# Attention and two feed-forward layers on one core: keys in groups of two token tiles, split left-over tokens, and a re-planned instruction order

## The chip, the cores and the metric

The kernel runs on one core of a Trainium2 chip. The metric is the time of one execution in device microseconds, lower is better; a kernel's time is the median of its runs. The profile is one execution, recorded by the hardware. In it PE is TensorE, PEld its weight loads, DVE VectorE, ACT ScalarE, POOL GpSimd, and SP the engine that issues most DMAs.

## The reference

Four batches, eight heads, 576 tokens, head size 64; then 2304 tokens of width 512 through two feed-forward layers of width 2048. Everything is float32.

```python
def phi(x):                                  # w_phi is 64 x 128
    proj = np.einsum('bhsd,df->bhsf', x, w_phi)
    proj = proj - np.max(np.abs(proj), axis=-1, keepdims=True)
    return np.concatenate([np.exp(proj), np.exp(-proj)], axis=-1)
q_p, k_p = phi(q), phi(k)
kv = np.einsum('bhsf,bhsd->bhfd', k_p, v);  z = np.sum(k_p, axis=2)
num = np.einsum('bhsf,bhfd->bhsd', q_p, kv)
den = np.einsum('bhsf,bhf->bhs', q_p, z)[..., None] + 1e-06
x = (num / den) as 2304 x 512
x = leaky_relu(x @ w_in1, 0.01) @ w_out1     # first layer
x = relu(x @ w_in2) ** 2 @ w_out2            # second layer
```

## The kernel before

**Number formats.** A product that needs float32 accuracy is made in one of two ways. *Plain*: one float32 matmul, which the trace shows as two records of the PE. *Split*: both operands are cut into a rounded "high" and a "low" part of type float32r, and three matmuls (high·high, low·high, high·low) replace the plain one. Layers one and two are split throughout; in the attention, `P["pk"]`, `P["pq"]` and `P["pn"]` say up to which batch the K projection, the Q projection and the numerator stay plain (0, 0 and 1). The products of K features with V ("kv") are always plain.

**Attention.** Work goes by pairs of heads, four pairs in a batch. `k_pair` loads a pair's keys (512 tokens of two heads stacked on 128 partitions, `kt`; the 64 left-over tokens of each head as one 64 x 128 tile, `krt`) and values (`vt`). It then passes over five groups: the left-over tile (number 4, one head's width of 128 columns for both heads) and the token tiles 0 to 3 (two heads, 256 columns). For each group PE projects into a PSUM bank (`proj`), DVE takes the largest magnitude of every row and negates it (`center`, tile `kmx`), ACT makes exp of the projection and of its negative, one instruction per head and sign, straight from the bank (`expo`, tile `kp`), and PE multiplies by V into the pair's accumulator (`kv`, bank 0, or 0 and 7 in batch 0). After batch 0 the K projections have one bank, number 1; the Q projections and numerators use banks 1 and 0. The accumulator is copied out (`kvf`) and split (`kvh`, `kvl`). `q_pair` does 288 query tokens of a pair: projection for each head (`proj`), copy out of the bank (`qps`), a largest magnitude over partitions on POOL (`qm`), exponentials (`qe`, split into `qeh` and `qel`), numerators and denominators of both heads (`numer`), evacuation (`qnum`, `qden`), reciprocal, product and split into the input `xr` of layer one.

**Layer one** runs over five blocks of tokens (four of 512, one of 256) and 16 chunks of the width 2048 (`moe`): twelve up-projection matmuls into bank 2 or 3 (`xr` with the weights in `arena` or `more`), leaky relu and split on ACT and DVE (`g`, `gh`, `gl`), and twelve down-projection matmuls into banks 4 to 7. The attention of batch b+1 is worked in between the chunks of earlier blocks. While these run, DVE and ACT also turn the weights, which arrive as 64-bit words, into split float32 (`raw`, `wf`), and prepare the second layer's weights (`stage_pair`). **Layer two** follows on PE alone with its own block scheme (`h_unit`, `y_unit`).

**What sets the order.** No engine is ordered by hand. Every piece of work is an `Op` of a `Plan`, with a cost for each engine that may do it, a position `pos`, and its operands. `Plan.order` plays these costs through: a free engine takes the ready operation with the smallest position whose tiles and banks are free. The instructions are then issued in the order in which the play started them, and each engine of the chip works through its list in that order. The positions come from the table `P`: `k0`, `kz`, `kp`, `ks`, `kvd` and others say where a K pair, its tiles and its kv products stand relative to the chunks; `stage0`, `stage`, `lead` and the like where weights are prepared. Between the end of an operation and the start of one that depends on it the play lays `lat`, 0.28, and nothing on the same engine:

```python
for o in op.next:
    t = now + (0.0 if op.engine in o.engines and len(o.engines) == 1 else self.lat)
```

While the play finds nothing for PE in the first 95 us (`fill`), it puts a small bfloat16 matmul on a tile of zeros there, whose result is not used.

Of the kernel before, what the change touches and what calls it, by code (L numbers as in the profile page):

```python
# [19 lines left out]
PAIRS = H // 2  # L20
# [23 lines left out]
EDGE = 24  # L44

P = dict(
    ring=6, wf=2, raws=3, k0=-115.69, kz=(-22.16, -25.13, -28.64), kp0=14.6, kp=22.44, ks=1.84, kvd=6.19, kb=0, pk=0, pq=0, pn=1, qk=2.73, qk2=13.5,
    q20=-8.75, qd=(3.27, -21.24, 20.79, 10.82, -2.12, -17.72, 26.78), wlead=30.91, wl0=-7.1, ydelay=16.3, xs=(174.51, 74.74, 10.17), xl=11.4, xk=4.78,
    xk2=8.22, xst=74.82, xld=24.14, lead=43.44, slead=-24.15, w2lead=29.72, ylead=53.84, evac=-12.29, stage0=-99.0, stage=14.29, stage2=-10.59,
    pl=-1.44, c_alt=43.95, sq_alt=7.93, klead=27.27, qlead=25.53, hi_alt=0.31, dve_alt=34.87, port=1.25, lat=0.28, issue=0.47, dma=2.5, rate=320e3,  # L50
    kvc=0.9, fill=95, cold=4.98, coldf=2.2,
# [29 lines left out]
class Plan:  # L81
# [30 lines left out]

    def order(self, filler=None):
        now, n_done, seq, port = 0.0, 0, 0, 0.0
# [6 lines left out]

        def make_ready(op):
            for e, (_, extra) in op.engines.items():
                heapq.heappush(ready[e], (op.pos + extra, id_of[op], op))
# [19 lines left out]
        while n_done < len(self.ops):  # L144
            for e in free:
                while free[e] <= now:
                    skipped, found = [], None
                    while ready[e]:
                        item = heapq.heappop(ready[e])
                        op = item[2]  # L150
                        if op.engine:
                            continue
                        if can(op):
                            found = op
                            break
                        skipped.append(item)
                    for item in skipped:
                        heapq.heappush(ready[e], item)
# [25 lines left out]
                    if e == "PE" and now < P["cold"]:  # L184
                        cost *= P["coldf"]
# [8 lines left out]
            while events and events[0][0] <= now:  # L194
                _, _, what, op = heapq.heappop(events)
                if what == "end":
                    n_done += 1
                    seq += 1
                    heapq.heappush(events, (now + self.lat, seq, "free slots", op))
                    for o in op.next:  # L200
                        t = now + (0.0 if op.engine in o.engines and len(o.engines) == 1 else self.lat)
                        seq += 1
                        heapq.heappush(events, (t, seq, "dep", o))
                elif what == "free slots":
                    for v in op.uses:
                        v.left -= 1
                        if not v.left and v.banks:
                            del held[v.bank]
# [9 lines left out]
def attention_moe_moe(ctx: ExitStack, tc: tile.TileContext, qd, kd, krd, vd, wpd, wd, out):  # L218
# [37 lines left out]
    for k in range(2):  # L256
# [50 lines left out]
    def new(tag, shape, dtype):  # L307
        pl, n = tags[tag]
        where = late() if pl == "b" else right() if pl == "r" else pools[pl]
        if tag == "kmx":  # L310
            return where.tile([128, LINE], dtype, tag=tag, name=tag, bufs=n + 1)[:, 0:4].rearrange("p (a b c) -> p a b c", a=2, b=2)
# [33 lines left out]
    def r_pass(n, ops=1):  # L345
        return ops * (n * 0.447e-3)
# [13 lines left out]
    def pe(c):  # L360
        return {"PE": (c, 0)}
# [224 lines left out]
    def moe(n):  # L586
# [29 lines left out]
        plan.add(pe(cost), pos, lambda e: h_part(e, 0), r=[*rd, win], w=[hb], after=before)  # L616
        moe_h[n] = plan.add(pe(cost), pos + N / HALF, lambda e: h_part(e, 2), r=[*rd, win], w=[hb])
# [30 lines left out]
        for d0 in (0, 2):  # L648
            plan.add(
                pe(cost), pos + d0 / 2 * N / HALF, lambda e, d0=d0: y_part(e, d0), r=[gh, gl, wout], w=yv[i][d0:d0 + 2]  # L650
# [414 lines left out]
    def k_pair(b, p, tpos):  # L1065
        plain, plain_n = b <= P["pk"], b <= P["pn"]
        bias = b >= P["kb"]
        kt, krt, vt = Value("kt"), Value("krt"), Value("vt")
        t = {}

        def get_k():
            t["k"] = new("kt", [128, 512], F32)
            nc.sync.dma_start(out=t["k"], in_=kd[b, p])

        def get_r():
            t["r"] = new("krt", [64, 128], F32)
            nc.sync.dma_start(out=t["r"], in_=krd[b, p])
# [6 lines left out]
        load(32768, tpos[0] - lead, get_r, w=[krt])  # L1084
        load(262144, tpos[0] - lead, get_k, w=[kt])
# [3 lines left out]
        else:  # L1089
# [3 lines left out]
            def hi(e):  # L1093
                t["kh"] = new("kh", [128, 512], F32R)
                copy(e, t["kh"], t["k"])

            def lo(e):
                t["kl"] = new("kl", [128, 512], F32R)
                sub(e, t["kl"], t["k"], t["kh"])

            plan.add(to_hi(512), tpos[0] - 2, hi, r=[kt], w=[kh])
            plan.add(to_lo(512), tpos[0] - 1.5, lo, r=[kt, kh], w=[kl])
        acc = Value(banks=[0, 7] if b == 0 else [0])
        for n, (tt, pos) in enumerate(zip((4, 0, 1, 2, 3), tpos)):
            m = 1 if tt == 4 else 2
            pr, mx, kp, u = trans(b, True), Value("kmx"), Value("kp"), {}

            def proj(e, tt=tt, m=m, pr=pr):
                o = banks[pr.bank][:, 0:m * 128]
                tok = slice(tt * 128, (tt + 1) * 128)  # L1110
# [342 lines left out]
```

## Time and profile before

| | |
|---|---|
| time, median of 3 runs | 986.59 us (985.16 to 988.12) |
| time of the profiled execution | 989.14 us, of which its span is 987.4 us |
| PE busy | 962.4 us, 97% of the span |
| PEld, DVE, ACT busy | 860.3, 785.1 and 562.4 us |
| TensorE clock granted, mean | 0.996 of full |

The span runs from the first to the last instruction of the program. The end of a matmul record is modelled, and records of neighbours overlap, so a gap in PE's busy time is a true wait, while what a matmul costs is read from the distance of one start to the next.

### The profile page before, as it was taken

Reading aid. Unit: us, or ns where it says so; the run is one execution under the profiler, and the core shown is the slowest. Engines: PE = TensorE matmul, PEld = TensorE weight load, DVE = VectorE, ACT = ScalarE, POOL = GpSimd, SP = SyncE. Lnnn points to the kernel's source line nnn. Section 1 sums busy time; section 2 is a strip of 40 time slices with the busy share of each in tenths; the row PEclk is TensorE's granted clock in tenths of the full one; section 3 lists DMA queues with packets and bytes.
Section 4 is the critical chain, followed back from the end, with each engine's and each line's share of the span. In section 5 each row is a group of like instructions: output and inputs, shape, how many; then the busy total and the mean of one; then the engine's idle time right before and its main releaser. Section 6 shows DMA issues by size and latency. Waiting matters only on the chain.

```text
span 987.4 us, 16601 instructions
## 1 busy us (share of the span) xinstructions
PE 962.4 (97%) x5855; PEld 860.3 (87%) x5855; DVE 785.1 (80%) x1678; ACT 562.4 (57%) x1325; POOL 90.8 (9%) x52
## 2 busy tenths in 40 slices
PE   9999999999999999999999999999999999999997
PEld 6788777778888788878888899999999999999996
DVE  6999999799999999996334421778997787888878
ACT  7987777777678887776333332343633434334342
POOL 2220111011110111110000000000000000200101
PEclk9999999999999999999999999999999999999999
DMA  8449999778988688892589589888975293918623
GB/s 266 150 158 292 293 296 319 266 248 269 308 307 285 211 289 299 327 317 81 214 310 336 184 292 328 318 341 281 303 291 210 111 362 146 276 17 306 153 76 64
DMA packets 90290, 244.37 MB, mean 247 GB/s; under 512 B 8032, under 2 KB 33504, under 8 KB 87136
## 3 DMA queue, kind: packets, MB, share of 16 engines
q1 hardware_dynamic: 86896, 239.12, 69.5%
q0 software_dynamic: 3312, 4.20, 3.0%
q8 instruction: 46, 0.75, 0.3%
q14 instruction: 36, 0.29, 0.1%
HBM read 166.48 MB, written 76.81 MB: 246 GB/s over the span
## 4 chain that ended last, share of the span: by engine, by line
PE 57%; DVE 30%; DMA 5%; ACT 4%; issue 3%; POOL 0%; SPq 0%; DVEq 0%; ACTq 0%
PE bank L324 57%; DVE qden L1318 3%; DMA raw<-wd 3%; DVE wf L459 2%; DVE s L333 2%; DVE room L333 2%; DVE gl L333 2%; DVE g L967 2%; DVE kmx L1125 1%; DVE qel L333 1%; DVE raw L454 1%; DMA wcd<-room 1%; DVE arena L333 1%; DVE qnum L1321 1%; DVE kmx L1127 1%
## 5 line engine op out<-in xcount | busy, mean ns | idle before, releaser
L324 PE MATMUL bank<-gh,arena 128*128 128x512 f32 (+1 forms) x640 | 202.5, 374 | 0.0
L324 PE MATMUL bank<-xr,arena 128*128 128x512 f32 (+1 forms) x720 | 164.2, 371 | 0.0
L333 DVE TENSOR_TENSOR gl<-g,gh 128x512 fp32r<-128x512 f32 (+2 forms) x176 | 94.1, 539 | 67.6 <-ACT gh L328 67.0
L324 PEld LDWEIGHTS bank<-xr,arena 128*128 128x128 f32 x720 | 123.9, 189 | 20.6
L324 PEld LDWEIGHTS bank<-gh,arena 128*128 128x128 f32 x640 | 117.4, 189 | 19.1
L324 PE MATMUL bank<-gl,arena 128*128 128x512 f32 (+1 forms) x320 | 118.4, 370 | 0.5 <-DVE gl L333 0.5
L1248 POOL PARTITION_ALL_REDUCE qm<-qps x32 | 73.9, 2311 | 389.2 <-ACT qps L328 252.1
L328 ACT ACTIVATE gh<-g 128x512 fp32r<-128x512 f32 (+2 forms) x168 | 83.6, 502 | 37.0 <-PE bank L324 33.8
L1139 ACT ACTIVATE kp<-bank,kmx 128x128 f32<-128x128 f32 x288 | 82.3, 372 | 26.5 <-DVE kmx L1127 22.6
L622 ACT ACTIVATE g<-bank 128x512 f32<-128x512 f32 (+1 forms) x80 | 44.0, 552 | 80.8 <-PE bank L324 80.0
L324 PE MATMUL bank<-xc,w 128*128 128x384 f32 x504 | 89.8, 335 | 0.1
L324 PEld LDWEIGHTS bank<-xc,w 128*128 128x128 f32 x504 | 87.0, 188 | 0.6 <-DVE g L811 0.4
L324 PE MATMUL bank<-arena,sc 128*128 128x256 f32 x648 | 85.5, 284 | 0.1
L324 PEld LDWEIGHTS bank<-arena,sc 128*128 128x128 f32 x648 | 80.6, 188 | 1.9 <-DVE sc L333 0.3
L328 ACT ACTIVATE sc<-s 128x512 fp32r<-128x512 f32 (+1 forms) x70 | 37.8, 540 | 74.0 <-DVE s L333 36.0
L324 PEld LDWEIGHTS bank<-vt,kp 128*128 128x128 f32 x576 | 71.5, 191 | 5.5 <-issue 1.5
L324 PE MATMUL bank<-vt,kp 128*128 128x65 f32 (+1 forms) x576 | 72.6, 271 | 0.8 <-ACT qnum L328 0.6
L324 PEld LDWEIGHTS bank<-gl,arena 128*128 128x128 f32 x320 | 60.6, 189 | 9.6 <-DVE gl L333 1.4
L333 DVE TENSOR_TENSOR sc<-s,sc 128x512 fp32r<-128x512 f32 (+1 forms) x96 | 51.6, 555 | 19.5 <-ACT sc L328 18.6
L811 DVE TENSOR_TENSOR g<-bank,g 128x384 f32<-128x384 f32 x72 | 40.0, 555 | 30.3 <-PE bank L324 24.3
L1318 DVE RECIPROCAL qden<-qden 128x288 f32<-128x288 f32 x32 | 62.2, 1945 | 0.8 <-ACT qden L1304 0.8
L324 PE MATMUL bank<-arena,gh 128*128 128x256 f32 x324 | 60.0, 282 | 0.0
(142 smaller groups left out, 1839.9 us busy)
## 6 DMA issues: line engine op xcount, KB each, us to landing
arena<-wsd SPq DMA_DIRECT2D x72, 512.0 KB, 5.3
raw<-wd SPq DMA_DIRECT2D x64, 512.0 KB, 5.1
xc<-xcd SPq DMA_DIRECT2D x28, 768.0 KB, 13.5
arena<-wcd SPq DMA_DIRECT2D x10, 1792.0 KB, 7.9
wsd<-arena SPq DMA_DIRECT2D x28, 512.0 KB, 6.3
wid<-room SPq DMA_DIRECT2D x24, 512.0 KB, 4.2
wcd<-room SPq DMA_DIRECT2D x24, 512.0 KB, 4.8
xcd<-xc SPq DMA_DIRECT2D x14, 768.0 KB, 10.4
```

What stands on the lines that cost most here:

```text
L324: nc.tensor.matmul(out=o, lhsT=lhsT, rhs=rhs, start=start, stop=stop, **kw)
L328: nc.scalar.activation(out=out, in_=in_, func=ACTF.Copy)
L333: ENG[e].tensor_tensor(out=out, in0=a, in1=b, op=ALU.subtract)
L454: nc.vector.tensor_scalar(out=low, in0=low, scalar1=29, scalar2=None, op0=ALU.logical_shift_right)
L459: nc.vector.scalar_tensor_tensor(out=t["f"].bitcast(I32), in0=high, scalar=3, in1=low, op0=ALU.logical_shift_left, op1=ALU.bitwise_or)
L622: nc.scalar.activation(out=t["g"], in_=banks[hb.bank][:, 0:N], func=ACTF.Prelu, alpha=0.01)
L811: nc.vector.tensor_tensor(out=t[o], in0=m(z), in1=t["a"], op=ALU.add)
L967: nc.vector.tensor_tensor(out=o, in0=a, in1=b, op=op)
L1125: nc.vector.tensor_reduce(out=mx[1], in_=o, axis=AX.X, op=ALU.max, apply_absolute_value=True)
L1139: nc.scalar.activation(out=u["kp"][:, s, h, :], in_=banks[pr.bank][:, h * 128:(h + 1) * 128], func=ACTF.Exp, scale=sg, bias=u["mx"][:, s, ...
L1248: nc.gpsimd.partition_all_reduce(out_ap=t["m"].rearrange("p h s -> p (h s)"), in_ap=t["ps"].rearrange("p h s -> p (h s)"), channels=128, r ...
L1318: nc.vector.reciprocal(out=t["d"], in_=t["d"])
```

## The change

It has three parts. **Groups:** in batches 1 to 3 the five groups of a K pair become three, (left-over tile and tile 0), (tiles 1 and 2) and (tile 3), with three, four and two heads in a bank; the tile `kp` doubles, and there is one `center` and one run of `expo` for each group. Batch 0 keeps five groups. **Left-over tokens:** they lie in `kt` behind the other 512, in the lower 64 partitions, so that one DMA brings both. In batches 1 to 3 they are projected split, with 256 columns, by three float32r matmuls of 64 rows, where a plain 128-column matmul did it. **Plan:** the one latency becomes five (`lat`, `self`, `of_pe`, `to_pe`, `far`); a layer-one operation (kind "m") on PE costs 0.096 more when the operation before it is of another kind, and PE stays with the kind that it is at when such work is ready within 2 positions; several costs and nearly all numbers of `P` are new. `vt` has one buffer where it had two, and `kvh` and `kvl` two where they had three.

```diff
+KGROUPS = (
+    tuple(((t,), k) for k, t in enumerate((4, 0, 1, 2, 3))),
+    (((4, 0), 0), ((1, 2), 2), ((3,), 4)),
+)
-    ring=6, wf=2, raws=3, k0=-115.69, kz=(-22.16, -25.13, -28.64), kp0=14.6, kp=22.44, ks=1.84, kvd=6.19, kb=0, pk=0, pq=0, pn=1, qk=2.73, qk2=13.5,
+    ring=6, wf=2, raws=3, k0=-165.76, kz=(-19.68, -14.1, -59.35), kp0=15.85, kp=18.51, ks=2.09, kvd=5.48, kb=0, pk=0, pq=0, pn=1, qk=4.25, qk2=11.43,
...
+    def lag(self, a, b):
+        if a == "PE" or b == "PE":
+            return 0.0 if a == b else P["of_pe"] if a == "PE" else P["to_pe"]
+        return P["far"] if "SP" in (a, b) or "POOL" in (a, b) else P["self"] if a == b else self.lat
...
+                    if e == "PE" and found and kind_of(found) != kind:
+                        rest = [i for i in ready[e] if i[2].engine is None and i[0] <= item0 + P["stick"] and kind_of(i[2]) == kind and can(i[2])]
+                        if rest:
+                            heapq.heappush(ready[e], (item0, id_of[found], found))
+                            item = min(rest)
...
+                        if op.engines[e][2] and op.engines[e][2] != kind:
+                            cost += P["switch"]
...
-        "kt": ("a", 2), "krt": ("a", 2), "vt": ("a", 2), "kh": ("a", 1), "kl": ("a", 1), "kmx": ("a", 3), "ksb": ("a", 1),
-        "kp": ("a", 2), "kvf": ("a", 1), "kvh": ("a", 3), "kvl": ("a", 3),
+        "kt": ("a", 2), "vt": ("a", 1), "kh": ("a", 1), "kl": ("a", 1), "kmx": ("a", 3), "ksb": ("a", 1),
+        "kp": ("a", 2), "kvf": ("a", 1), "kvh": ("a", 2), "kvl": ("a", 2),
...
-        load(32768, tpos[0] - lead, get_r, w=[krt])
-        load(262144, tpos[0] - lead, get_k, w=[kt])
+        load(327680, tpos[0] - lead, get_k, w=[kt])
...
-                if tt == 4:
-                    mm(o, t["r"], wst[0:64, 0:128], True, True)
-                elif plain:
-                    mm(o, t["k"][:, tok], wst[:, 128:384], True, True)
-                else:
-                    mm(o, t["kh"][:, tok], wbh, True, False)
-                    mm(o, t["kl"][:, tok], wbh, False, False)
-                    mm(o, t["kh"][:, tok], wbl, False, True)
+                for y, tt in enumerate(reversed(tiles)):
+                    sl, rows, n = (slice(512, 640), slice(0, 64), 128 if plain else 256) if tt == 4 else (slice(tt * 128, (tt + 1) * 128), slice(0, 128), 256)
+                    ws = [w[rows, 0:n] for w in (wst[:, 128:384], wbh, wbl)]
+                    o = banks[pr.bank][:, 256 * y:256 * y + n]
+                    if plain:
+                        mm(o, t["k"][rows, sl], ws[0], True, True, skip_group_check=True)
+                    else:
+                        mm(o, t["kh"][rows, sl], ws[1], True, False, skip_group_check=True)
+                        mm(o, t["kl"][rows, sl], ws[1], False, False, skip_group_check=True)
+                        mm(o, t["kh"][rows, sl], ws[2], False, True, skip_group_check=True)
...
-            plan.add(pe(P["kvc"] if m == 2 else 0.45), pos + P["kvd"], kv, r=[kp, vt], w=[acc])
+            plan.add(pe((P["kvc"] + 0.02 * (m > 2)) * m), pos + P["kvd"] + P["ks"] * (len(tiles) - 1), kv, r=[kp, vt], w=[acc])
```

**Left-over tokens on PE.** Before, in batch 1 to 3, a plain left-over projection (`wst,krt`) stands alone between float32r matmuls; here down-projections of layer one (`gh,arena`) are ahead of it and behind the Q projection (`qs,arena`). One of the 12 places:

```order
L324 MATMUL bank_80<-gh,arena 128x512
L324 MATMUL bank_80<-gl,arena 128x512
L324 MATMUL bank_80<-gh,arena 128x512
L324 MATMUL bank_76<-wst,krt 128x128
L324 MATMUL bank_75<-qs,arena 128x288 x2
L324 MATMUL bank_81<-gh,arena 128x512
```

After the change, the first group of such a pair is six float32r matmuls into bank 1 (`bank_76`), tile 0 first and then the left-over tile; `xr,arena x6` is half an up-projection of layer one:

```order
L348 MATMUL bank_77<-xr,arena 128x512 x6
L348 MATMUL bank_76<-qs,arena 128x288 x2
L348 MATMUL bank_77<-xr,arena 128x512 x6
L348 MATMUL bank_76<-room,kh 128x256
L348 MATMUL bank_76<-room,kl 128x256
L348 MATMUL bank_76<-room,kh 128x256 x2
L348 MATMUL bank_76<-room,kl 128x256
L348 MATMUL bank_76<-room,kh 128x256
L348 MATMUL bank_79<-gh,arena 128x512
```

The plain matmul is gone from these batches, and three float32r ones stand in its group.

**The first numerators of batch 2 on PE.** Before, the last kv products of the pair (`vt,kp`) are followed by the two Q projections of the next queries, with six up-projection matmuls behind each, and then by the first numerator (`qeh,kvh`), which needs the kv products copied out and split:

```order
L324 MATMUL bank_75<-vt,kp 128x65 x4
L324 MATMUL bank_76<-qs,arena 128x288 x2
L324 MATMUL bank_78<-xr,arena 128x512 x6
L324 MATMUL bank_76<-qs,arena 128x288 x2
L324 MATMUL bank_78<-xr,arena 128x512 x6
L324 MATMUL bank_76<-qeh,kvh 128x288
```

Now one Q projection, six up-projection and twelve down-projection matmuls (banks 4 to 7, `bank_79` to `bank_82`) stand between the last kv products and that numerator; above the first row here are `bank_75<-vt,kp 128x65 x4`, the Q projection, the six up-projections and one down-projection:

```order
L348 MATMUL bank_79<-gl,arena 128x512
L348 MATMUL bank_79<-gh,arena 128x512
L348 MATMUL bank_80<-gh,arena 128x512
L348 MATMUL bank_80<-gl,arena 128x512
L348 MATMUL bank_80<-gh,arena 128x512
L348 MATMUL bank_81<-gh,arena 128x512
L348 MATMUL bank_81<-gl,arena 128x512
L348 MATMUL bank_81<-gh,arena 128x512
L348 MATMUL bank_82<-gh,arena 128x512
L348 MATMUL bank_82<-gl,arena 128x512
L348 MATMUL bank_82<-gh,arena 128x512
L348 MATMUL bank_76<-qeh,kvh 128x288
```

The distance from the last kv product to the numerator grew from twelve 512-column matmuls and two Q projections to eighteen and one, and the second Q projection of the pair moved behind the numerators.

## Rows read from the trace of the kernel before

**Rows 1.** The page: the span of the profiled execution.
```profile
span 987.4 us, 16601 instructions
```

**Rows 2.** Stretch, its length, busy PE, PEld, DVE, ACT, POOL, clock, DMA share, GB/s.
```profile
0.00:73.50 73.50, 70.66 (x497) 56.00 (x498) 63.10 (x139) 61.86 (x185) 19.81 (x14) 1.00 0.59 190
73.50:460.00 386.50, 374.14 (x1960) 310.56 (x1960) 361.80 (x717) 292.81 (x733) 52.12 (x22) 1.00 0.83 282
460.00:950.00 490.00, 487.10 (x3154) 463.97 (x3153) 330.91 (x751) 194.58 (x381) 15.21 (x13) 1.00 0.70 241
```

**Rows 3.** Waits of PE, 73.5 to 460: us in total, times, longest.
```profile
PE bank L324 <- ACT kp L1139: 3.7, 5, 1.2
PE bank L324 <- DVE kvh L330: 1.9, 1, 1.9
PE bank L324 <- ACT qps L328: 1.9, 4, 0.8
PE bank L324 <- ACT qden L1304: 1.7, 5, 0.5
```

**Rows 4.** Timeline of PE around one left-over projection: start, length, instruction.
```profile
292.73 0.39 PE L324 MATMUL bank<-gh,arena 128*128 128x512 f32 x1
293.05 0.49 PE L324 MATMUL bank<-wst,krt 64*128 64x128 f32 x2
293.46 0.50 PE L324 MATMUL bank<-gh,arena 128*128 128x512 f32 x1
293.80 0.39 PE L324 MATMUL bank<-gl,arena 128*128 128x512 f32 x1
294.03 0.62 PE L324 MATMUL bank<-gh,arena 128*128 128x512 f32 x2
```

**Rows 5.** Timeline of PE: a split K projection and its kv products.
```profile
280.73 0.29 PE L324 MATMUL bank<-room,kh 128*128 128x256 f32 x1
...
281.10 1.00 PE L324 MATMUL bank<-vt,kp 128*128 128x65 f32 x8
281.90 1.63 PE L324 MATMUL bank<-xr,arena 128*128 128x512 f32 x6
283.37 0.40 PE L324 MATMUL bank<-gh,arena 128*128 128x512 f32 x1
...
284.76 0.29 PE L324 MATMUL bank<-room,kh 128*128 128x256 f32 x1
```

**Rows 6.** Timeline of PE: sixteen kv records in one run.
```profile
54.37 1.90 PE L324 MATMUL bank<-vt,kp 128*128 128x65 f32 x16
56.10 0.61 PE L324 MATMUL bank<-zeros 128*128 128x128 bf16 x8
```

**Rows 7.** Timeline of PE: a wait for the bank of a Q projection.
```profile
152.09 0.53 PE L324 MATMUL bank<-qs,arena 128*128 128x288 f32 x2 [0.78 <-ACT qps L328]
152.46 0.39 PE L324 MATMUL bank<-gh,arena 128*128 128x512 f32 x1
```

**Rows 8.** Timeline of PE: the first numerators of batch 2.
```profile
221.81 0.37 PE L324 MATMUL bank<-qeh,kvh 128*128 128x288 f32 x1 [1.92 <-DVE kvh L330]
222.44 0.61 PE L324 MATMUL bank<-qeh,kvl 128*128 128x288 f32 x1 [0.26 <-DVE kvl L333]
```

**Rows 9.** Those numerators, columns as in rows 2.
```profile
222.00:225.00 3.00, 2.74 (x11) 2.56 (x11) 2.51 (x5) 0.41 (x1) 0.00 (x0) 0.53 0.24 49
```

**Rows 10.** Timelines of DVE and ACT behind the K projection at 280.73.
```profile
281.69 0.42 DVE L1125 TENSOR_REDUCE kmx<-bank 128x2 f32<-128x256 f32 x1
...
282.41 1.14 ACT L1139 ACTIVATE kp<-bank,kmx 128x128 f32<-128x128 f32 x4
```

**Rows 11.** Groups of DVE by form: count, busy us, mean ns, idle before.
```profile
L1125 DVE TENSOR_REDUCE kmx<-bank 128x2 f32<-128x256 f32 x64 | 26.3, 411 | 5.2 <-PE bank L324 5.0
...
L1125 DVE TENSOR_REDUCE kmx<-bank 128x1 f32<-128x128 f32 x16 | 4.4, 273 | 1.1 <-PE bank L324 1.0
```

**Rows 12.** Timeline of PE: the first up-projection.
```profile
73.56 2.77 PE L324 MATMUL bank<-xr,arena 128*128 128x512 f32 x11
```

More of the change, by code (lines that the diff above doesn't have):

```diff
@@ L197, in order @@
                     n_done += 1
-                    seq += 1
-                    heapq.heappush(events, (now + self.lat, seq, "free slots", op))
+                    for v in op.uses:
+                        seq += 1
+                        heapq.heappush(events, (now + (self.lag(op.engine, "PE") if v.banks else P["of_pe"]), seq, "free", v))
                     for o in op.next:
-                        t = now + (0.0 if op.engine in o.engines and len(o.engines) == 1 else self.lat)
                         seq += 1
[L203 to L208, printed above, removed]
+                        heapq.heappush(events, (now + self.lag(op.engine, next(iter(o.engines))), seq, "dep", o))
+                elif what == "free":
+                    if isinstance(op, Value):
+                        op.left -= 1
+                        if not op.left and op.banks:
+                            del held[op.bank]
                 elif what == "dep":
@@ L310, in new @@
         if tag == "kmx":
[L311 removed]
+            return where.tile([128, LINE], dtype, tag=tag, name=tag, bufs=n + 1)[:, 0:8].rearrange("p (a b c) -> p a b c", a=2, b=4)
         if tag == "vt":
@@ L1132, in expo @@
-            def expo(e, m=m, pr=pr, u=u):
-                u["kp"] = new("kp", [128, 2, 2, 128], F32)
-                for s, sg in ((0, 1.0), (1, -1.0)):
-                    if not bias:
-                        nc.scalar.activation(out=u["kp"][:, s, 0:m, :], in_=u["sb"], func=ACTF.Exp, scale=sg)
-                        continue
-                    for h in range(m):
+                nc.vector.tensor_scalar(out=mx[0], in0=mx[1], scalar1=-1.0, scalar2=None, op0=ALU.mult)
+            def expo(e, m=m, pr=pr, u=u):
+                u["kp"] = new("kp", [128, 2, 4, 128], F32)
+                for h in range(m):
+                    for s, sg in ((0, 1.0), (1, -1.0)):
@@ L1158, in k_pair @@
-            if bias:
-                plan.add({"DVE": (m * 128 * 1.04e-3 + 0.25, 0)}, pos + 0.4, center, r=[pr], w=[mx]).shared = False
-                plan.add({"ACT": (0.5 * m, 0)}, pos + 0.8, expo, r=[pr, mx], w=[kp])
-            else:
-                sb = Value("ksb")
-                plan.add({"DVE": (on_dve(m * 128, 2) + 0.12, 0)}, pos + 0.4, center, r=[pr], w=[sb, mx]).shared = False
-                plan.add(acts(m * 128, ops=2), pos + 0.8, expo, r=[sb], w=[kp])
-            plan.add(pe(P["kvc"] if m == 2 else 0.45), pos + P["kvd"], kv, r=[kp, vt], w=[acc])
+            cost = sum((0.415 if plain else 0.36) if tt == 4 else 0.536 if plain else 0.36 for tt in tiles)
@@ L1166, in k_pair @@
+            plan.add(pe(cost), pos, proj, r=[wsv, kt] if plain else [wcv, *ksrc], w=[pr])
+            plan.add({"DVE": (m * 128 * 1.04e-3 + 0.25, 0)}, pos + 0.4, center, r=[pr], w=[mx]).shared = False
+            plan.add({"ACT": (0.5 * m, 0)}, pos + 0.8, expo, r=[pr, mx], w=[kp])
+            plan.add(pe((P["kvc"] + 0.02 * (m > 2)) * m), pos + P["kvd"] + P["ks"] * (len(tiles) - 1), kv, r=[kp, vt], w=[acc])
         pos = tpos[-1] + P["kvd"] + 0.1
```

100 lines of the change are left out of this document (49 added, 51 removed).

## The prediction

> **What bounds the kernel now.** I read the busy times first, then PE's waits, then PE's timeline, because in this kernel each answers only part of the question. The span is 987.4 us [rows 1]; the profiled execution took 989.14, so 1.7 us lie outside it, and it was 2.55 us above the median of 986.59. I work out differences against the span and subtract them from the median.
>
> By stretches [rows 2], three parts stand apart. Until 73.5 us layer one cannot start, since its input comes from the attention of batch 0; the first up-projection is at 73.56 [rows 12]. From there to 460 the attention of batches 1 to 3 and the weights' conversion run beside layer one: PE is without a matmul for 386.5 - 374.14 = 12.4 us, and DVE is busy for 361.8 of 386.5, 94%. From 460 to 950 PE lacks 2.9 us in 490. So PE is the wall everywhere, and what is to be won without taking matmuls away lies nearly all in the middle stretch, where DVE is almost as full.
>
> The waits of that stretch [rows 3] name what PE stood for: K exponentials (3.7 us in 5 waits), one wait of 1.9 for the copied kv products, banks of Q projections and numerators (`qps` and `qden`, 3.6 in 9). A wait also costs a little behind it: of the two Q projections after the wait at 152.09 the next matmul starts 0.37 later [rows 7], where by the 0.37 of three 256-column matmuls [rows 5] two of 288 columns would need 2 x 0.37 / 3 x 288 / 256 = 0.28; I take 0.1 for each wait. And the clock answers once: after the wait at 221.81 [rows 8] the granted clock is 0.53 over 3 us [rows 9], that is, close to the lower of its two levels, 1.2 GHz; 3.00 x 0.47 = 1.4 us are lost there beyond the wait itself.
>
> **Left-over tokens.** A matmul of 512 columns starts 0.23 after its neighbour (293.80 to 294.03, [rows 4]). From the matmul ahead of the plain left-over projection to the second one behind it, 292.73 to 293.80, it takes 1.07; less two pitches that is 0.61 for the one plain matmul, with what its change of format costs on both sides. Three float32r matmuls of 256 columns take 281.10 - 280.73 = 0.37 [rows 5]. There are 12 such places in batches 1 to 3. The new matmuls have only 64 rows, which no row shows; I take the full-height price, because it is the nearest row of the same format and column count, and keep no gain (0.61) as the other end. The sum is 12 x (0.61 - 0.37) = **2.9 us less**, bounds 0 and 2.9. The page "TensorE: Matmul & The Clock Gate" of the Trainium skill (section "Why this matters for your kernels") says that a matmul of few rows takes the time of one of all 128; by that too the price would be 0.37.
>
> The wider `kt` makes `kl` a quarter longer on DVE and adds one smaller DMA less per pair; both lie beside PE work, and would show only as later K projections.
>
> **Fewer changes of kind.** The plan charges 0.096 when PE comes to layer one from other work, and the new order has fewer such changes: I count 122 stretches of layer-one matmuls before and 92 after. At face value that is 30 x 0.096 = 2.9 us. The trace does not bear it out. Eight kv records take 0.80 (281.10 to 281.90), and the six matmuls behind them 1.47, 0.09 above six pitches [rows 5]: 0.89 in all, or 0.111 a record. Sixteen in one run take 1.73 [rows 6], or 0.108. What is lost at the end of a short run is nearly won at its beginning. I take **0** for it, with 0.003 for each of the 576 kv records, 1.7 us, as the other end.
>
> **The waits.** Here the order decides, and I price only what can be read from it.
>
> The wait at 221.81: between the last kv products of the pair and its first numerator stood twelve 512-column matmuls, 12 x 0.23 = 2.8, and two Q projections, and PE waited 1.92 and, for the low half, 0.26 [rows 8]. Now it is eighteen matmuls, 4.1 us. That leaves some 0.6 to 0.9 of the wait, if the engines behind it are as late as before, and lateness was the unusual part: the view has one such wait [rows 3], for 16 pairs. I take it as gone, with the low clock: **3.7 us less** (1.9 + 0.3 + 0.1 + 1.4), bounds 0 and 3.7.
>
> Banks 0 and 1: in the old order 34 Q projections or numerators are followed in their own bank by the next user after only six 512-column matmuls, 1.4 us of PE work, in which ACT or DVE must copy the bank out. In the new order there are 17. The copy's own length is a third of that; what is late is the queue ahead of it on ACT. `qps` and `qden` cost 3.6 us in 9 waits [rows 3] and 0.9 behind them. Half of 4.5, rounded up for the waits of the same sort on `qnum` that the view has below these rows: **2.5 us less**, bounds 0 and 5.
>
> The K groups: fewer and larger. A two-head group went like this [rows 5, 10]: projection finished at 281.10, maximum on DVE from 281.69, exponentials on ACT from 282.41 for 1.14, bank 1 free at 283.55, next projection into it at 284.76. That left 1.2 us. A four-head group adds 2 x (0.411 - 0.273) = 0.28 to the maximum [rows 11] and four more exponentials, 1.0 to 1.1; bank 1 is free 1.3 later. The new order puts a median of 4.35 us of PE work between such a group and the bank's next user, where 284.76 - 281.10 = 3.66 stood here: 1.2 + 0.7 - 1.3 leaves 0.6. So 11 groups after the start become tighter by 0.6, while there are 36 hand-overs of bank 1 where there were 60. I leave the 3.7 us of waits for exponentials [rows 3] as they are: **0**, bounds 2 less and 7 more (11 x 0.6). The page "ScalarE: Activation LUTs" of the Trainium skill (section "What ACT_TABLE_LOAD costs") gives 280 ns and 0.833 ns a column for an activation with a bias from memory, 93 ns of it overlapped; eight of 128 columns would be 2.4 by this estimate, against 2.2 from the row, and the 0.6 would be 0.4.
>
> **The start.** 26 more fill matmuls are planned (209 against 183). At 0.61 for eight, an upper price [rows 6], that is 2.0 us; kv products, K and Q projections of batch 1 worth 2.8 us (16 records at 0.11, six float32r matmuls at 0.12, two at 0.14) are moved ahead of layer one, and those come off later. PE already lacked 73.5 - 70.66 = 2.8 us there [rows 2], in which some of the fill will lie. **0.7 more**, bounds 1 less and 4 more.
>
> **Layer two** keeps its order but for a few rows, and its 2.9 us of waits [rows 2]: **0**, bounds 2 either way. `vt` with one buffer delays the next pair's values until the last kv product of the pair before has run; the load then has most of a pair's spacing, 18 us in the new plan, so I price it at 0; without that cover, each pair's first kv products would wait for a load.
>
> The sum: -2.9 - 3.7 - 2.5 + 0.7 = -8.4 us, so a span near 979 and a time of 986.6 - 8.4 = **978.2**.
>
> **Rivals.** *The waits move instead of going* (no measurable change). An order made with other latencies has its tight places elsewhere; for this speaks that the kv products of the last three pairs of batch 1 now have 1.6 to 1.9 us before their numerators, where two of them had 3.0 and 3.3. Only the left-over tokens would pay, less the start: 986.6 - 2.9 + 0.7 to 2 = 984 to 986.
>
> *DVE becomes the bound* (slower). The last kv products stand 37 us of PE work earlier than before, so the attention's DVE work is packed more tightly, and DVE had only 24.7 us to spare in 386.5 [rows 2]. Counted over both orders with the mean length of each form (rows as in [rows 11]), DVE has 5 to 7 us more to do ahead of the places between 275 and 375 us of PE work. If the spare time is all unusable (it was idle while ACT or PE had yet to deliver), PE waits those 7 us more, and the four-head groups take 4 to 7 of their own: 986.6 - 2.9 + 0.7 + 7 = 991. It decides from the point where DVE's busy share in the middle stretch passes 96%. Against it: fewer maxima and negations, 56 of each for 80, and 13 fewer copies of `qps` and `qnum` on DVE.
>
> *Nearly all middle waits go.* 12.4 idle, 2 behind the waits and 1.4 of low clock are 16; with the left-over tokens 19: 967.6.
>
> **How the numbers follow.** My forecast 0.50 (own range 971 to 984), waits move 0.22, DVE bound 0.14, all waits gone 0.14. A measurement of this kernel tells 0.3%, 3 us, from no change, so faster means under 983.6. That takes in nearly all of the forecast, the last rival and a little of the first: 0.66. Same, 983.6 to 989.5: 0.21. Slower: 0.13. The range 968 to 990 leaves out about half of each of the two outer rivals.
>
> **What would show it.** Left-over tokens: no `wst,krt` rows after 75 us, and about 0.37 for three 64-row matmuls. Waits: PE's idle time in the stretch up to the end of the attention falls from 12.4 to about 6, no stretch at a clock near 0.5 around the first numerators of batch 2, and `qps` and `qden` at half. Kind: kv runs at 0.11 a record whatever their length. I am wrong if waits for `kp` grow past 7 us, if DVE is over 96% busy there, or if the first up-projection comes after 77 us.

## The result and the profile after

The changed kernel took 976.5 us (median of 4 runs, 974.6 to 977.65), the kernel before 986.98 beside it: ratio 0.9884, interval [0.9863, 0.9906], 10.5 us less at these medians. The forecast was 978.2. The profiled execution took 976.32. Its page:

```profile
span 974.6 us, 16578 instructions
```

The same stretches as in [rows 2], cut where the new kernel begins layer one. Columns: stretch, its length, busy PE, PEld, DVE, ACT, POOL, clock, DMA share, GB/s.

```profile
0.00:77.70 77.70, 74.69 (x547) 61.06 (x548) 67.78 (x142) 65.60 (x197) 20.89 (x14) 1.00 0.60 198
77.70:460.00 382.30, 375.89 (x1994) 316.42 (x1993) 362.93 (x686) 293.78 (x737) 55.31 (x23) 1.00 0.82 282
460.00:950.00 490.00, 487.93 (x3204) 467.32 (x3203) 325.19 (x748) 194.20 (x374) 12.76 (x12) 1.00 0.71 245
```

In the middle PE now lacks 382.3 - 375.89 = 6.4 us, where it lacked 12.4 [rows 2]; DVE is busy for 95% of it, where it was 94%. The waits of PE in that stretch (us in total, times, longest), beside [rows 3]:

```profile
PE bank L348 <- ACT kp L1151: 2.6, 4, 1.0
PE bank L348 <- ACT qps L352: 1.5, 2, 1.3
PE bank L348 <- ACT qden L1312: 1.2, 2, 1.0
```

No wait for `kvh` is left in the view. `kp` went from 3.7 to 2.6, `qps` and `qden` together from 3.6 in 9 waits to 2.7 in 4. The first numerators of batch 2 stood behind a wait of 1.92 at clock 0.53 [rows 8, 9]; in PE's timeline of the new kernel they follow layer one's matmuls at once, and the clock of that stretch is full:

```profile
215.29 0.39 PE L348 MATMUL bank<-gh,arena 128*128 128x512 f32 x1
215.52 0.29 PE L348 MATMUL bank<-qeh,kvh 128*128 128x288 f32 x1
215.65 0.30 PE L348 MATMUL bank<-qeh,kvl 128*128 128x288 f32 x1
```
```profile
214.00:219.00 5.00, 5.00 (x30) 4.44 (x29) 4.83 (x10) 2.56 (x6) 0.00 (x0) 1.00 0.93 316
```

Two places divide the span into three: the first up-projection (`xr`, 512 columns) and layer two's first matmul (`xc`). PE's timeline after, and then the one row of before that is not among [rows 12]:

```profile
77.68 1.55 PE L348 MATMUL bank<-xr,arena 128*128 128x512 f32 x6
...
602.64 0.86 PE L348 MATMUL bank<-xc,w 128*128 128x384 f32 x4
```
```profile
612.01 1.21 PE L324 MATMUL bank<-xc,w 128*128 128x384 f32 x6
```

The start is 77.68 - 73.56 = 4.1 us **longer**. The middle is 524.96 long, where it was 612.01 - 73.56 = 538.45: **13.5 less**. Layer two and the end are 974.6 - 602.64 = 372.0 where they were 375.4: **3.4 less**. Together -12.8, the difference of the two spans. The two profiled executions differ by 2.3 more than the medians do.

### The profile page after: what moved, and what is told of

It reads as the page before. It is cut to its first block, busy times and chain, and to the rows that moved or that the text cites. A ratio compares the mean times of both kernels' runs of the same rounds, so it can differ in the third digit from the quotient of the medians.

```text
span 974.6 us, 16578 instructions
## 1 busy us (share of the span) xinstructions
PE 957.0 (98%) x5893; PEld 862.9 (89%) x5893; DVE 775.2 (80%) x1628; ACT 562.0 (58%) x1327; POOL 92.6 (9%) x52
## 4 chain that ended last, share of the span: by engine, by line
PE 56%; DVE 31%; DMA 6%; issue 3%; ACT 3%; SPq 0%; DVEq 0%; ACTq 0%
PE bank L348 56%; DVE qden L1326 3%; DVE s L357 3%; DVE gl L357 2%; DMA raw<-wd 2%; DVE wf L483 2%; DVE room L357 2%; DVE g L991 1%; DVE kmx L1144 1%; DVE raw L478 1%; DVE g L835 1%; DMA wid<-room 1%; DVE qm L357 1%; DMA wsd<-arena 1%; DVE qs L357 1%
## 5 line engine op out<-in xcount | busy, mean ns | idle before, releaser
L348 PE MATMUL bank<-gh,arena 128*128 128x512 f32 (+1 forms) x640 | 200.1, 372 | 0.0
L352 ACT ACTIVATE gh<-g 128x512 fp32r<-128x512 f32 (+2 forms) x157 | 77.5, 501 | 38.6 <-PE bank L348 35.2
L1151 ACT ACTIVATE kp<-bank,kmx 128x128 f32<-128x128 f32 x288 | 79.9, 382 | 16.0 <-DVE kmx L1145 14.2
L348 PE MATMUL bank<-arena,sc 128*128 128x256 f32 x648 | 83.3, 282 | 0.2 <-DVE g L839 0.2
L352 ACT ACTIVATE sc<-s 128x256 fp32r<-128x256 f32 (+1 forms) x89 | 45.9, 517 | 62.8 <-DVE s L357 23.7
L348 PE MATMUL bank<-vt,kp 128*128 128x65 f32 (+1 forms) x576 | 70.4, 273 | 1.6 <-ACT qden L1312 1.0
L352 ACT ACTIVATE g<-bank 128x384 f32<-128x384 f32 (+2 forms) x60 | 29.0, 483 | 57.6 <-PE bank L348 57.6
```

Of the source, the lines that this page charges most:

```text
L348: nc.tensor.matmul(out=o, lhsT=lhsT, rhs=rhs, start=start, stop=stop, **kw)
L352: nc.scalar.activation(out=out, in_=in_, func=ACTF.Copy)
L1151: nc.scalar.activation(out=u["kp"][:, s, h, :], in_=banks[pr.bank][:, h * 128:(h + 1) * 128], func=ACTF.Exp, scale=sg, bias=u["mx"][:, s, ...
```

## The experiments

Twelve kernels ran, in three sets. The kernel before, measured beside each set, stood at 988.23, 987.7 and 988.57, so I compare ratios: 0.9884 is the changed kernel.

### The left-over tokens

The plain place cost 0.61 us [rows 4]; the new one should have cost 0.37. PE's timeline of the changed kernel around one (the `x2` holds the last matmul of 128 rows and the first of 64):

```profile
220.81 0.59 PE L348 MATMUL bank<-room,kh 128*128 128x256 f32 x2
221.25 0.27 PE L348 MATMUL bank<-room,kl 64*128 64x256 f32 x1
221.36 0.28 PE L348 MATMUL bank<-room,kh 64*128 64x256 f32 x1
221.57 0.50 PE L348 MATMUL bank<-gh,arena 128*128 128x512 f32 x1
221.90 0.39 PE L348 MATMUL bank<-gl,arena 128*128 128x512 f32 x1
```

From 220.81 to 221.90 are 1.09 us; less one pitch of 256 columns (0.12) and one of 512 (0.23) that is 0.74 for the three, dearer than the plain one. Either small row counts cost, or the change between 64 and 128 rows does. `left_full` lets them read all 128 rows (the added rows of the keys are zeros):

```diff
-  sl, rows, n = (slice(512, 640), slice(0, 64), 128 if plain else 256) if tt == 4 else ...
+  sl, rows, n = (slice(512, 640), slice(0, 128), 128 if plain else 256) if tt == 4 else ...
```

> The changed kernel, same instructions in the same order; only the left-over projections take all 128 rows of the key tile and of the weights (the added rows of the keys are zeros) instead of 64. Theory A, row height: in the changed kernel's trace the three 64-row matmuls of a left-over projection are surrounded by longer pitches (0.210 ahead, 0.222 at the first, 0.205 at the last, 0.335 behind, against 0.118, 0.118, 0.118 and 0.227), 0.39 us a place, because PE passes from 128-row to 64-row weights and back. With full rows these go: 12 x 0.39 = 4.7 us less, 971.8. Theory B, the extra belongs to the second half of the bank or to the end of an accumulation: pitches stay, 976.5.

Ratio 0.9901 [0.988, 0.9921], 977.31 us: no gain. The same place in its timeline:

```profile
223.22 0.40 PE L348 MATMUL bank<-room,kh 128*128 128x256 f32 x2
223.45 0.28 PE L348 MATMUL bank<-room,kl 128*128 128x256 f32 x1
223.57 0.28 PE L348 MATMUL bank<-room,kh 128*128 128x256 f32 x1
223.69 0.39 PE L348 MATMUL bank<-gh,arena 128*128 128x512 f32 x1
223.92 0.40 PE L348 MATMUL bank<-gl,arena 128*128 128x512 f32 x1
```

From 223.22 to 223.92 are 0.70, so 0.35 for the three: 0.39 less at each of 12 places, 4.7 us of PE's work, and nothing of it in the time. Its waits from 72 to 460 have grown by as much, from 6.5 us in all to 11.2:

```profile
PE bank L348 <- ACT kp L1151: 3.9, 6, 1.1
PE bank L348 <- ACT qps L352: 3.7, 3, 1.8
PE bank L348 <- ACT qden L1312: 2.5, 4, 1.5
```

(This profiled execution was 4.8 us above its kernel's median, so the waits are more than typical.) `left_full_128` takes full rows and 128 columns, and `before_left_full` gives the kernel before, with its plain left-over projection, 128 rows (the upper 64 zero):

```diff
-  sl, rows, n = (slice(512, 640), slice(0, 64), 128 if plain else 256) if tt == 4 else ...
+  sl, rows, n = (slice(512, 640), slice(0, 128), 128) if tt == 4 else ...
```

> As the run with full rows, and the left-over projections are 128 columns wide instead of 256 (the other 128 are not used by anything). If a float32r matmul's pitch follows its columns, each goes from 0.118 to 0.06: 36 x 0.058 = 2.1 us less than with 256 columns, 969.7. Rival: narrow float32r matmuls are slower, or the weight load sets the pitch: same as with 256 columns, 971.8, or up to 4 us more.

```diff
-  t["r"] = new("krt", [64, 128], F32)
+  t["r"] = new("krt", [128, 128], F32)
...
-  mm(o, t["r"], wst[0:64, 0:128], True, True)
+  mm(o, t["r"], wst[:, 128:256], True, True)
...
```

> The kernel before, same order, its plain left-over projection with 128 rows (64 of them zeros). Theory A, row height: the 0.61 that a place costs is 2 x 0.11 for the two records, as for kv products of 128 columns, and the rest is the change of rows; 12 x 0.37 = 4.4 us less, and up to 1 us in the start: 982 to 982.5. Theory B, change of number format (the theory of the prediction): stays at 0.61 a place, 986.9.

They gave 0.9893 [0.9874, 0.9912] and 0.9993 [0.9981, 1.0005]. The profiled execution of `left_full_128`, 2.2 us below its median, has less to show: PE's waits from 72 to 460 are 7.9 us in all, and its middle is 523.8, 1.2 less. The kernel before shows the same cost of height. Its place with 128 rows, in the timeline:

```profile
324.11 0.38 PE L324 MATMUL bank<-wst,krt 128*128 128x128 f32 x2
324.25 0.48 PE L324 MATMUL bank<-gh,arena 128*128 128x512 f32 x1
324.56 0.40 PE L324 MATMUL bank<-gl,arena 128*128 128x512 f32 x1
```

From 324.11 to 324.56 are 0.45, less one pitch of 0.23: 0.22 for what took 0.61 with 64 rows. So it was never the number format: going from matmuls over 128 rows to matmuls over 64 and back costs some 0.39 a place, whichever the format. Three times it was taken away, and three times the time stayed.

`q_full` does the same for batch 0's plain Q projections, which lie before layer one begins:

```diff
-  mm(o, wst[0:64, 0:128], t["q"][0:64, h, :], True, True)
+  mm(o, wst[:, 128:256], t["q"][:, h, :], True, True)
```

> The changed kernel, same order; the 16 plain Q projections of batch 0 take 128 rows (weights with 64 zero rows) instead of 64. Their records then have the pitch of the plain numerators of as many columns, 0.242 for 0.333: 32 x 0.09 = 2.9 us less PE time ahead of the first up-projection. If PE sets the pace of the start, 973.6; if chains through DVE, ACT and POOL set it, the waits there grow by as much and the time stays at 976.5 (between the two is likely: 975).

0.9886 [0.9871, 0.99]. The first up-projection is at 77.58, as good as unmoved, though the 32 records, from start to start and without recorded waits, take 1.35 us less: the start is not set by PE's matmuls alone either.

### Parts of the change undone

Four kernels undo one rule each. The first has five groups again in batches 1 to 3, the second the one old latency, the third no preference for layer one ("stick") and no price for a change of kind, the fourth no fill matmuls after 5 us.

```diff
-    (((4, 0), 0), ((1, 2), 2), ((3,), 4)),
+    tuple(((t,), k) for k, t in enumerate((4, 0, 1, 2, 3))),
```

> The changed kernel with its planner and its table of numbers, but five K groups a pair in all batches (left-over projection still split, 64 rows). Theory G, the grouping itself pays, because each group costs ACT a wait for DVE's maximum (ACT's waits for kmx in the middle stretch were 19.7 us in 25 before and 9.4 in 12 after): these waits come back to about 20 us, PE's gaps in the middle to 10 to 12, time 982 to 986. Theory L, the order planned with other latencies and numbers pays: 976 to 979. The numbers were not tuned for five groups, so a loss of 1 to 2 us alone tells nothing.

```diff
-        if a == "PE" or b == "PE":
-            return 0.0 if a == b else P["of_pe"] if a == "PE" else P["to_pe"]
-        return P["far"] if "SP" in (a, b) or "POOL" in (a, b) else P["self"] if a == b else self.lat
+        return 0.0 if a == b else 0.28
```

> The changed kernel, groups and numbers as they are, but planned with the old latency (0.28 between engines, 0 on the same). Theory L, the latencies themselves pay, since the order they give leaves PE more work between a bank's copy and its next use: PE's gaps in the middle go from 6.4 back to 10 to 12 us, 981 to 984. Rival, the groups or the numbers pay and the latencies hardly move the order: 975 to 978.

```diff
-    ... switch=0.096, ...
+    ... switch=0.0, ...
-                    if e == "PE" and found and kind_of(found) != kind:
+                    if False:
```

> The changed kernel planned without the price of a change of kind on PE and without staying with a kind. By the plan's own price, 0.096 for each change, about 30 changes more would cost 2.9 us: 979.4. By the trace's rows a change costs nothing (kv runs of 8 and of 16 records both 0.11 a record): 976.5, within 2 us either way for the other order.

```diff
-    ... fill=95, ...
+    ... fill=5, ...
```

> The changed kernel, same order, without the fill matmuls after the first 5 us of the plan (some 170 of 209 left out). If they delay the attention of batch 0, 0.056 each, the first up-projection comes up to 9 us earlier and the time falls to 967. If they lie in waits that are there anyway, nothing changes: 976.5. If without them the clock falls in the gaps of the start, the plain matmuls there take longer, the first up-projection comes 1 to 4 us later: 977.5 to 980.5. I hold the last for likeliest.

| kernel | time, us | ratio to before |
|---|---|---|
| five_groups | 997.17 | 1.0099 [1.0074, 1.0124] |
| old_lag | 991.53 | 1.0031 [1.0016, 1.0045] |
| no_stick | 989.6 | 1.0014 [0.9999, 1.0029] |
| no_fill | 991.18 | 1.0035 [1.0019, 1.005] |

All four came out above every range that I had written down for them. Each lost 1.3% or more of the time against the changed kernel, 13 us and up, so the losses cannot be added up to the gain. For two of them the profile shows a place. In `five_groups` PE's waits for K exponentials are four times those of the changed kernel (73 to 475 us):

```profile
PE bank L348 <- ACT kp L1151: 10.8, 6, 3.5
```

`no_fill` was to keep the order and did not (PE's rows without the fills differ in more than a thousand places), so it compares two orders. Its clock does show that the fills are gone: from 60 to 80 us PE is busy half the time and was granted 0.81, where the changed kernel, with its fills, has 1.00:

```profile
60.00:80.00 20.00, 9.58 (x34) 6.73 (x34) 17.65 (x31) 15.19 (x42) 4.59 (x3) 0.81 0.43 153
```

Its first up-projection comes at 85.93, 8.2 us later; how much of that is the clock and how much the other order is not shown.

`no_stick` is of another sort. PE's waits from 600 us on, its timeline where layer two begins, and ACT's there:

```profile
PE bank L348 <- ACT xc L352: 11.3, 1, 11.3
PE bank L348 <- DVE gl L357: 2.5, 1, 2.5
```
```profile
602.54 0.69 PE L348 MATMUL bank<-xc,w 128*128 128x384 f32 x3
614.52 0.69 PE L348 MATMUL bank<-xc,w 128*128 128x384 f32 x1 [11.30 <-ACT xc L352]
```
```profile
613.95 0.52 ACT L352 ACTIVATE xc<-xt 128x384 fp32r<-128x384 f32 x1 [5.01 <-DMA xt<-x2d]
```

Its layer two begins at 602.54, as in the changed kernel (602.64). The whole loss is one stall behind it: layer two's input comes back through memory (`x2d`), and no matmul of layer one's last block was left to cover that. The changed kernel has 48 of them (256 columns each) behind layer two's first matmul, the kernel before 36. The rule helped by what it happened to leave for the end. About the price of a change of kind the run says nothing: counted as in the prediction, its order has 95 stretches of layer-one matmuls, hardly more than the 92 of the changed kernel, where some 30 more were expected. It is the groups that make these stretches fewer, since `before_groups` (below) has 98 without the rule, and `five_groups` 118 with it.

### Is it the order itself?

Two kernels ask how good an order is that nothing was fitted to: `shifted` moves one number of the table a little, `before_groups` has the groups and the split left-over tokens with the planner's rules and all shared numbers as before.

```diff
-    ... kp=18.51, ...
+    ... kp=18.7, ...
```

> A control. The changed kernel with one number of the table moved a little: kp=18.51 becomes 18.7, a shift of 0.19 us of where the planner wants the K projections of batches 1 to 3; 655 rows of PE's stream then stand otherwise, and nothing else changes. Theory tuned order (what the perturbed plans lost, 13 to 20 us, is largely the loss of an order that the table's numbers were fitted to, and says little about the part that was undone): 981 to 990. Rival (any order of this planner is about as good, and the losses of the other runs belong to the part undone): 974.5 to 978.5.

```diff
-    ... lat=0.125, self=0.115, of_pe=0.2, to_pe=0.46, far=0.28, switch=0.096, stick=2.0, ...
+    ... lat=0.28, switch=0.0, stick=0.0, ...       # and the shared numbers of the old table
...
+        return 0.0 if a == b else 0.28
...
```

> The K groups and the split left-over alone: the changed kernel's code with the planner's rules and all shared numbers of the table as they were before (one latency of 0.28 for every step, no switch, no stick); only the three numbers that the groups need are new. Theory groups pay by themselves: 978 to 984. Rival, tuned order (the gain came with an order fitted to new rules, and the groups in the old table's order find it no better than any unfitted order): 988 to 997.

`shifted` took 984.88 us, 0.9955 [0.9936, 0.9974]: 0.19 us in one position cost 0.7%, some 7 us. (Its profiled execution took 3330 us, far from the other nine, so its profile is not read.) `before_groups` took 990.6, 1.0031 [1.0008, 1.0055]: not faster than before. Its first up-projection is at 80.36 and layer two's first matmul at 610.92, a middle of 530.6. The theory of the tuned order held in both. An order that nothing was fitted to cost 7 us in `shifted`, the one run that undoes nothing: two thirds of what the change gains. `before_groups` lies 15 us above the changed kernel, but it leaves out the planner's rules as well, so it is not a control alone. `old_lag`, `no_stick` and `no_fill` lie at 13 to 15 us, `five_groups` at 21; how much of each is the part undone, no run tells.

One thing can be read from the profiled executions. Against the kernel before, `before_groups` is 7.9 us shorter in the middle (530.6 for 538.45). Some 2.7 of that only moved (8 kv records and three K matmuls to the start, twelve last-block matmuls to layer two). So the groups and the split left-over tokens, without the new rules, did gain in the middle; the order lost it again in the start (80.36 for 73.56) and in layer two (377.4 for 375.4).

### Is it DVE?

Why does PE's time in the middle not count? DVE is at 95% there. `light` keeps the order and leaves out the true denominators, so that its output is not the reference's: DVE's reciprocal falls from 1.95 to 0.15 us, 1.8 less in each of 32 blocks. `light_left_full` adds the edit of `left_full`.

```diff
-  nc.scalar.activation(out=t["d"][o:o + 64], in_=..., func=ACTF.Copy, bias=EPS)
+  nc.scalar.activation(out=t["d"][o:o + 64], in_=..., func=ACTF.Copy, scale=0.0, bias=1e-8)
...
-  nc.vector.reciprocal(out=t["d"], in_=t["d"])
+  nc.vector.tensor_scalar(out=t["d"][:, 0:1], in0=t["d"][:, 0:1], scalar1=1.0, scalar2=None, op0=ALU.mult)
```

> The changed kernel in the same order, with the denominators written as one constant by their eviction (the products are computed and not used) and DVE's reciprocal over 288 columns cut to one column: output not the reference's. It takes some 1.9 us from DVE in each of 32 blocks, 25 of them in the middle, where DVE is at 95%. Theory DVE paces the middle (PE's waits there come from DVE's queue running full): the middle's 6.4 us of PE's waits fall to 1 or 2, total 969 to 972. Rival, latency (the waits are chains through a bank's product, ACT and back, which DVE's load does not set): 974 to 977.

> Both edits, the constant denominators with the one-column reciprocal, and the left-over projections with all 128 rows of keys as in the run left_full (the rows past the tile's end are other keys, whose products go unread): output not the reference's. Theory DVE paces the middle (what full rows save on PE was given back as waits only since DVE was full): below the run before it by the 4.5 us that the pitches lose, 964 to 968. Rival, latency: within 1 us of the run before it.

(The added rows are zeros here too, as in `left_full`, not other keys.)

`light` took 970.42 us, 0.9823 [0.9797, 0.9848], as the theory of DVE had it; DVE is busy for 328.14 of the 383 us from 72 to 455, 86%, and PE's waits there are down to two lines:

```profile
PE bank L348 <- ACT kp L1151: 1.6, 2, 1.0
PE bank L348 <- ACT qps L352: 1.3, 1, 1.3
```

`light_left_full` took 967.79, 0.9798 [0.9772, 0.9823], 2.6 us less. By this number alone the theory of DVE would hold, at the edge of its range (964 to 968). The timelines show something else; first `light`, then `light_left_full`:

```profile
79.46 0.85 PE L348 MATMUL bank<-xr,arena 128*128 128x512 f32 x3
...
596.71 0.51 PE L348 MATMUL bank<-xc,w 128*128 128x384 f32 x2
```
```profile
75.86 0.85 PE L348 MATMUL bank<-xr,arena 128*128 128x512 f32 x3
...
593.84 0.69 PE L348 MATMUL bank<-xc,w 128*128 128x384 f32 x3
```

The middle is 517.25 in the one and 517.98 in the other. The difference of these two executions lies wholly in the start, where `light` ran at a clock of 0.79 from 10 to 20 us and 0.87 from 20 to 30, and the other at 1.00. So even with DVE relieved, cheaper left-over projections were not worth anything in the middle of these two: PE's waits there are 2.9 us in `light` and 5.9 in `light_left_full`. One such place can be followed. ACT's timeline in `light_left_full`, in `left_full`, and the first of the two rows in `light`:

```profile
214.21 0.63 ACT L352 ACTIVATE room<-s 128x512 fp32r<-128x512 f32 x1 [1.98 <-DMA wid<-room]
214.74 0.39 ACT L352 ACTIVATE qps<-bank 128x288 f32<-128x288 f32 x1
```
```profile
221.90 0.63 ACT L352 ACTIVATE room<-s 128x512 fp32r<-128x512 f32 x1 [2.93 <-DMA wid<-room]
222.43 0.39 ACT L352 ACTIVATE qps<-bank 128x288 f32<-128x288 f32 x1
```
```profile
217.85 0.63 ACT L352 ACTIVATE room<-s 128x512 fp32r<-128x512 f32 x1 [1.21 <-DMA wid<-room]
```

The copy that frees the bank of a Q projection (`qps`) stands on ACT behind a piece of weight conversion, and that waits until a transfer has emptied its buffer. PE's next K projection, into that bank, waited 0.84 us in the first and 1.79 in the second, and 0.17 in the changed kernel. Counted from the first up-projection, that step begins 138.4 us later in `light` (217.85 - 79.46) and in `light_left_full` (214.21 - 75.86) alike, though PE has less to do in the second: when PE comes earlier, the transfer doesn't. Whether all the waits that took the place of the saved work are of this sort is not settled; that they are not DVE's load alone is.

## Why the prediction was right, point by point

**Where the time is.** The forecast had the gain in the middle's waits, and part of it is there: PE's gaps went from 12.4 to 6.4 (about 6 was forecast), 6 of the middle's 13.5 us. The sum was right within 2 us, and that was luck in part. As measured below, the terms in the forecast's order come to 1.6 + 0 - 3.7 - 1.4 - 1.1 + 1.3 - 3.4 = -6.7 us, where -8.4 was forecast: the left-over tokens were 4.5 worse, and layer two, put at nothing, was 3.4 better. The other 6.1 of the 12.8 between the two spans came from what no term covered.

**Left-over tokens, forecast -2.9: wrong in sign.** The step that failed is "I take the full-height price, because it is the nearest row of the same format and column count". The place went from 0.61 to 0.74, not to 0.37: 12 x 0.13 = 1.6 us more, since a change of the row count costs at both ends. My upper end, 0.61, left that out. The other half of the mistake was to put the 0.61 down to "its change of format": with 128 rows the plain place takes 0.22. I also let a saving on PE count in full in the stretch with PE's waits; three runs saved 4.7 us each there and gained nothing.

The page "TensorE: Matmul & The Clock Gate" of the Trainium skill, which I had weighed (section "Why this matters for your kernels"), says a matmul of few rows costs what one of 128 does. By it the price was 0.37; the trace has 0.74 with 64 rows and 0.35 with 128. Between two matmuls of 64 rows the trace agrees (221.25 to 221.36, 0.11, where 128 rows take 0.12); the extra lies where the row count changes.

**Kind changes, 0: held.** In the middle 35 of layer one's 512-column matmuls stood directly behind kv records and started the next one some 0.09 late; now 13 do, 2.1 us less. The kv records take that back: there are 16 fewer of 65 columns in the middle, worth 1.8, yet all kv records of the middle together take 0.4 more from start to start.

**The wait at 221.81 and its clock, -3.7: held.** Both are gone.

**`qps` and `qden`, -2.5: mis-sized.** Their waits fell by 0.9 us and 5 occasions, some 1.4 with the 0.1 behind each.

**K groups, 0: held within its bounds.** `kp` lost 1.1 us. The eight exponentials brought no more waiting; ACT's own waits for the maximum became fewer, with fewer maxima. The two lines of ACT's waits, before (73.5 to 460) and after (73 to 460):

```profile
ACT kp L1139 <- DVE kmx L1127: 19.7, 25, 2.5
```
```profile
ACT kp L1151 <- DVE kmx L1145: 9.4, 12, 1.6
```

**The start, +0.7: held, though its sign of error came.** The first up-projection is 4.1 us later, past the 77 us that I had named. But 2.8 of that is the work moved ahead of layer one, which the forecast let come off later and which the middle no longer has. So 1.3 stands against 0.7, inside the bounds. That the idle time would take some of the fill was wrong: from start to start the fills take 14.6 us where they took 12.3, and PE's recorded waits in the start went from 1.7 to 1.9.

**Layer two, 0: mis-sized.** It was -3.4, beyond the bound of 2, and that with the 1.4 us of last-block matmuls that moved behind layer two's first. PE's waits in it fell by 0.9; where the rest went is not followed.

**What no term covered.** Between layer one's first and layer two's first matmul, the starts of its 1536 matmuls of 512 columns, with idle time taken off, sum to 362.7 us before and 357.0 after (0.236 and 0.232 each, by the starts of the timeline). Of these 5.7 us, 2.1 are those behind kv records, which the kv records take back, and about 1 is the long pitch behind the plain left-over projection, which moved to the split ones. The rest are delays too short for the view of waits. Numerators, summed in the same way, take 2.2 us less; of this some 1.4 is the low clock, in my -3.7 already, which fell on them. They start 0.24 apart there, from 222.44 to 225.25, where 0.13 is usual; in PE's timeline before:

```profile
222.85 0.45 PE L324 MATMUL bank<-qel,kvh 128*128 128x288 f32 x1
223.09 0.45 PE L324 MATMUL bank<-qeh,kvh 128*128 128x288 f32 x1
223.33 0.45 PE L324 MATMUL bank<-qeh,kvl 128*128 128x288 f32 x1
```

PE's waits on lines other than those named fell by 1.7, from 2.4 to 0.7. And the 1.4 us of last-block matmuls left the middle. My reading priced the named waits only.

**The rivals.** That the gain does not show is what became of the unfitted `before_groups` (1.0031), though there the start and layer two took it, not the middle's waits. That DVE bounds the middle is half right: it stood at 95%, just under the 96% I had given, and taking 1.8 us a block from it gave 6 us at the medians.

What stays open: how the 10.5 us divide between groups and plan. Any kernel that undoes a part also has an order that nothing was fitted to, and that alone cost 7 us in the one control.

## What to carry to other kernels

Where engines work in step, price a saving on one of them by the waits behind it: if the next bank is freed by another engine or by a transfer, the saved time can come back as a wait, as it did here. Before undoing a part of a planned kernel to see its worth, shift the plan by something that should not matter; here 0.19 us in one position cost 7 us, which is the size of effect below which such a comparison says nothing. Read a matmul's price from rows between the same neighbours, with the same height as well as the same format. And when a forecast hits, add up its terms as measured: here the total was near while half of the gain lay outside of them.

## What was new about the hardware

Matmuls over 64 rows (both operands on 64 partitions) between matmuls over 128 cost PE 0.39 us a place, plain (0.61 against 0.22) and split (0.74 against 0.35) alike; the extra lies in the start distances at both ends. Halving the columns of the three full-height matmuls saved little: in `left_full_128` the place takes 220.86 to 221.54 in its timeline, 0.68 against 0.70, since of the narrow ones only the first is followed sooner (0.06), the other two still 0.11 later, and layer one's first matmul behind them takes 0.28 instead of 0.23:

```profile
220.86 0.34 PE L348 MATMUL bank<-room,kh 128*128 128x256 f32 x2
221.04 0.27 PE L348 MATMUL bank<-room,kl 128*128 128x128 f32 x1
221.15 0.28 PE L348 MATMUL bank<-room,kh 128*128 128x128 f32 x1
221.26 0.45 PE L348 MATMUL bank<-gh,arena 128*128 128x512 f32 x1
221.54 0.39 PE L348 MATMUL bank<-gl,arena 128*128 128x512 f32 x1
```
